# Handing over the recurrent states in the third quarter of six steps of a gated-attention and MLP kernel

## The chip, the core and the metric

The kernel runs on one core of a Trainium2 chip. The metric is the device time of one execution in microseconds. Several executions of each kernel are timed, and their median is what counts. A separate execution is recorded by the hardware profiler, and that is where the rows below come from.

## What is computed

The reference is a gated linear attention followed by an MLP with a SiLU:

```python
for t in range(S):
    state = alpha[:, :, t, :, None] * state + np.einsum('bhd,bhe->bhde', k[:, :, t], v[:, :, t])
    y[:, :, t] = np.einsum('bhd,bhde->bhe', q[:, :, t], state)
# x: y with its heads side by side, (B*S, H*D)
h = x @ w_in
g = h * (1.0 / (1.0 + np.exp(-h)))
out = g @ w_out
```

Here B = 4 batches, H = 8 heads, S = 768 time steps and D = 48. The MLP has 3072 tokens, a model width of 384 and an inner width of 2048. The weights come as 64-bit floating point numbers and are turned into 32-bit ones on the chip.

## The kernel before

**Chunks.** The time axis is cut into 6 chunks of 128 steps for each of the 4 batches, which makes 24 chunks (n = 0 to 23; n counts batches first, so chunk n + 4 continues chunk n). Each chunk goes through four stages:

- `products` (L710): transposes the chunk's decays, keys and queries on TensorE (L729), copies the decays (L731), and lets VectorE run what the prediction calls the chain: a scan (L734), the smallest decays (L737), the scaled keys kp (L745), a reciprocal (L762), a second scan (L764) and the scaled queries p (L770).
- `scores` (L792): kp times p on TensorE into two PSUM tiles, copied by ScalarE (L812) and masked by GpSimd (L813, in later steps L825); kp is also transposed into kn (L830, L832).
- `values` (L843): the masked scores g times v, and from the second chunk of a batch on p times the state, into a PSUM tile which ScalarE copies to `xt` (L863), the input of the MLP.
- `states` (L864): kn times v in 16 small matmuls (L874), put into the state of the batch: copied by ScalarE for a batch's first chunk (L882), added by VectorE afterwards (L880).

**Steps.** A loop (L1203) runs 25 steps of four quarters. In step s the quarters hold scores of chunk s-1, products of chunk s, values of chunk s-1 and states of chunk s-1. From step 8 on (`NA`) they are grouped differently. Behind states of chunk n two more things are issued: `load(n + 3)`, the decays, keys and queries of a later chunk (L477), and `load_v(n + 2)` (L501), both from SyncE's queue. Each quarter ends with `fill(step, slot)` (L1184), which lays down as much of the MLP's work as is due by then.

**The MLP's work** comes in pieces (generators). In the first steps these are `enter_plain` (L911), two column blocks of `x @ w_in` each, 6 matmuls into a `ps_m` bank and a Silu by ScalarE (L923); later `leave` (L1035), which multiplies by w_out and by differences of its blocks (`wt`). Ahead of pieces, `fill` has the weights converted: `weights` (L614) takes slices of 128 x 512 of w_in (12 slices) and 128 x 384 of w_out (16 slices). A slice's raw bits are fetched by SyncE's queue (L519) into one of four buffers, rounded by ScalarE (L629) and put together by VectorE in three instructions (L645, L646, L647). A new fetch is issued behind each conversion, and waits for its buffer.

**What sets the order.** The Python code gives a program order. A scheduler of the framework lays down, when the kernel is built, one fixed order for each engine: in program order by priority, but an instruction that it reckons ready may go ahead of one that it reckons is still waiting. On the chip each engine keeps to that order and waits on semaphores. Thus a stage that is moved in the program can change the order on all engines around it, also of instructions that the edit doesn't name. Matmul lines all show as L388, transposes as L392, because a small wrapper records them.

Of the kernel before, what the change touches and what calls it, by code (L numbers as in the profile page):

```python
# [355 lines left out]
def quotients(  # L356
# [98 lines left out]
    NA = 2 * GB  # L455
# [10 lines left out]
    def load(n, names="akq"):  # L466
        if n == NT:
            return
        c = ctxs.setdefault(n, dict(zip(("ci", "b"), divmod(n, B))))
        b, rows = c["b"], slice(c["ci"] * C, c["ci"] * C + C)  # L470
        for name, src in (("a", alpha), ("k", k), ("q", q)):
            if name not in names:
                continue
            x = src[b, :, rows, :]
            if n < NA:
                c[name] = nat[name][n % NIN]
                nc.sync.dma_start(c[name][:, :, 0:D], x.transpose([1, 0, 2]))  # L477
                continue

            c[name] = late["quads"][name]
            for u in range(2):
                for i in range(2):
                    r = 64 * u + 32 * i
                    nc.sync.dma_start(
                        c[name][r : r + 32, 32 * (1 - i) :][:, 0 : 4 * NP * D].rearrange(
                            "p (g c) -> p g c", g=NP),
                        x[u::2].rearrange("h (b j) d -> b h (j d)", j=4))
# [6 lines left out]
    def load_v(n):  # L496
        c = ctxs.setdefault(n, dict(zip(("ci", "b"), divmod(n, B))))
        x = v[c["b"], :, c["ci"] * C : c["ci"] * C + C, :].transpose([1, 0, 2])
        t = c["v"] = vns[n % NV]
        if n < NA:  # L500
            nc.sync.dma_start(t[:, :, 0:D], x)  # L501
            return
        nc.sync.dma_start(t[:, 0 : H // 2, 0:D], x[:, 0 : H // 2])
        for e in range(2):
            nc.sync.dma_start(t[CH * e : CH * e + CH, H // 2 :, 0:D], x[CH - CH * e : C - CH * e, H // 2 :])
# [665 lines left out]
    def settle():  # L1171

        first.close()
        late.update(look=pool("look"), part=pool("part"), turn=pool("turn"),
                    xc=pool("xc").tile([128, len(SUMS_X), TB], F32, name="xc"),
                    wx=pool("wx").tile([128, 8, NQ, 128], F32, name="wx"))
        quads = pool("quads")
        late["p"] = pool("p").tile([128, NP * W + 1], F32, name="p")
        late["quads"] = {name: quads.tile([128, 32 + 4 * NP * D], F32, name=f"{name}t") for name in "akq"}
        for name, t in late["quads"].items():  # L1180
            gps.memset(t, 1.0 if name == "a" else 0.0)
        load(NA)

    def fill(step, slot):  # L1184

        at = step * SLOTS + slot
        if at < marks[0]:
            if at == SLOTS:
                next(conv[0])
            elif step >= 1:  # L1190
                convert(0, (at - SLOTS) * 3 // (marks[0] - SLOTS) + 1)
            return
        i = next(i for i, m in enumerate(marks[1:]) if at < m)
        a, b = [work_at[n] for n in ([0] + phases)[i : i + 2]]
        due = a + (b - a) * (at - marks[i] + 1) / (marks[i + 1] - marks[i])
        if at % 2 == 0 and step > 3 * GB + 2:
            next(audits, None)
        while work_at[done + 1] <= due and pieces[done][2] <= bridged:
            convert(0, 3 * (done // 2) + 6)
            convert(1, 3 * (done - 6) // 2)  # L1200
            go_on()

    for step in range(STEPS):  # L1203
        if step == 1:
            load(NIN)
        stages = [[(scores, 1)], [(products, 0)], [(values, 1)], [(states, 1)]]
        if step == 1:

            stages = stages[1::-1] + stages[2:]
        elif step >= NA:  # L1210
            stages = [[(land, 1), (scores, 1)], [(products, 0)], [(quotient, 0)],
                      [(values, 1), (states, 1), (flip, 0)]]
        for slot, group in enumerate(stages):
            for stage, lag in group:
                n = step - lag
                if not 0 <= n < NT:
                    continue
                stage(n)
                if stage is values:
                    bridged = n + 1  # L1220
                if stage is states and n + 1 + NIN < NA:
                    load(n + 1 + NIN)
                if stage is states and n + NV < NT:
                    load_v(n + NV)
            if step * SLOTS + slot == (NA + 1) * SLOTS - 1:
                x = decayed.rearrange("p (o i c) -> p o i c", o=2, c=C)
                for r, o in later:
                    gps.memset(x[r, o, :, 0:CH], 0.0)
            fill(step, slot)
            if step * SLOTS + slot >= NA * SLOTS - 1 and conv_done[1] == NFT and not late:  # L1230
                settle()
# [32 lines left out]
@with_exitstack  # L1264
def kernel(
    ctx: ExitStack,
    tc: tile.TileContext,
    q: bass.AP,
    k: bass.AP,
    v: bass.AP,  # L1270
    alpha: bass.AP,
    moe_w_in: bass.AP,
    moe_w_out: bass.AP,
    out: bass.AP,
):


    flag = ctx.enter_context(tc.tile_pool(name="flag", bufs=1))
    small = flag.tile([1, 1], I32, name="small")
    args = (q, k, v, alpha, moe_w_in, moe_w_out, out)  # L1280
    within = quotients(tc, small, *args)
    with tc.If(within < 1, label="general"):
        general(tc, *args)
# [30 lines left out]
```

## Time and profile before

| | us |
|---|---|
| median of 3 runs (556.4 to 557.57) | 556.86 |
| the profiled execution | 557.26 |
| its span, first to last instruction | 555.5 |
| TensorE matmuls busy | 541.4 (97%) |
| TensorE weight loads busy | 489.7 (88%) |
| VectorE busy | 445.4 (80%) |
| ScalarE busy | 208.5 (38%) |
| GpSimd busy | 76.1 (14%) |

The mean granted TensorE clock is 0.999. In the rows, PE is TensorE's matmuls, PEld its weight loads, DVE VectorE, ACT ScalarE, POOL GpSimd and SPq SyncE's queue of DMA issues. A row of the timeline gives the start in us from the span's start, the time in us, the engine, the line, the operation, the tiles written and read with their shapes, how many instructions were merged into it, and in brackets how long the engine stood idle before it and what released it. A row of the waits gives an engine, its tile and line, what it waited for, and the sum in us, the number of times and the longest. A matmul of 32-bit numbers shows as two records, so 6 matmuls are a row of x12 and 16 of x32.

### The profile page before, as it was taken

The page shows a single profiled execution, that of the slowest core. Times are in us where ns is not written, and L with a number is a line of the kernel's source. Part 1 is how long each engine was busy: PE and PEld are TensorE (multiplying, and loading weights), DVE is VectorE, ACT ScalarE, POOL GpSimd, SP SyncE. Part 2 cuts the span into 40 slices and gives each one's busy share as a digit, 9 for nine tenths or more (in the row PEclk, how much of TensorE's full clock was granted, in tenths as well). Part 3 has the DMA queues.
Part 4 walks back from the last instruction along what each step waited for, and adds up shares of the span by engine and source line. Part 5 has one row for each costly group of instructions (what it writes and reads, how often), then busy time and mean ns, then how long its engine had stood idle before and what let it go on. Part 6 is the DMA issues. An engine that isn't in the chain of part 4 may idle for free. (4 is left out here: it accounts for less than half of the span.)

```text
span 555.5 us, 12640 instructions
## 1 busy us (share of the span) xinstructions
PE 541.4 (97%) x5026; PEld 489.7 (88%) x5026; DVE 445.4 (80%) x801; ACT 208.5 (38%) x466; POOL 76.1 (14%) x146
## 2 busy tenths in 40 slices
PE   6999999999999999999999999999999999999996
PEld 4788887998899999899999999988998999999996
DVE  5897788974999899997998986998884796945431
ACT  2556653223333253353353353344263342332100
POOL 3210000222210212021011021021121000001000
PEclk9999999999999999999999999999999999999999
DMA  9998971164454625355545654617642135500000
GB/s 215 246 249 210 232 195 33 47 161 116 117 136 125 159 63 138 86 145 149 139 112 139 193 139 120 191 27 183 170 137 91 54 91 169 172 11 22 10 24 30
DMA packets 99217, 70.09 MB, mean 126 GB/s; under 512 B 56272, under 2 KB 88656, under 8 KB 99152
## 3 DMA queue, kind: packets, MB, share of 16 engines
q1 hardware_dynamic: 97232, 65.30, 45.1%
q0 software_dynamic: 1920, 3.93, 2.0%
q8 instruction: 40, 0.66, 0.5%
q14 instruction: 25, 0.20, 0.1%
HBM read 61.34 MB, written 7.86 MB: 125 GB/s over the span
## 5 line engine op out<-in xcount | busy, mean ns | idle before, releaser
L388 PE MATMUL ps_o<-w_out,g 128*128 128x192 f32 x768 | 134.0, 328 | 0.5 <-DVE o L1056 0.5
L388 PEld LDWEIGHTS ps_o<-w_out,g 128*128 128x128 f32 x768 | 125.6, 190 | 3.5 <-DVE o L1056 1.0
L388 PE MATMUL ps_m<-xt,w_in 128*128 128x256 f32 x480 | 113.6, 383 | 1.5 <-ACT xt L863 1.1
L388 PEld LDWEIGHTS ps_m<-xt,w_in 128*128 128x128 f32 x480 | 89.1, 190 | 14.4 <-ACT xt L863 1.6
L388 PE MATMUL ps_o<-wt,g 128*128 128x192 f32 x576 | 99.7, 326 | 0.0
L388 PEld LDWEIGHTS ps_o<-wt,g 128*128 128x128 f32 x576 | 95.1, 190 | 1.6 <-issue 0.2
L388 PE MATMUL ps_m<-xc,w_in 128*128 128x256 f32 x288 | 70.7, 382 | 0.0
L388 PEld LDWEIGHTS ps_m<-xc,w_in 128*128 128x128 f32 x288 | 53.7, 190 | 7.0 <-DVE g L958 0.3
L1047 DVE TENSOR_TENSOR g<-g 128x512 f32<-128x512 f32 x72 | 50.1, 709 | 8.3 <-PE ps_o L388 8.3
L955 ACT ACTIVATE g<-g 128x1024 f32<-128x1024 f32 x32 | 33.1, 1056 | 61.2 <-DVE g L958 61.1
L1059 POOL DMA_DIRECT2D out_dram<-o x40 | 22.0, 551 | 219.5 <-DVE o L1056 113.7
L825 POOL TENSOR_SCALAR_AFFINE_SELECT g<-g 64x256 f32<-64x256 f32 x64 | 34.9, 546 | 124.4 <-ACT g L818 105.7
L388 PE MATMUL ps_m<-xc,wx 128*128 128x256 f32 x192 | 50.1, 383 | 1.0 <-DVE xc L586 1.0
L950 ACT COPY g<-ps_m 128x512 f32<-128x512 f32 x64 | 36.6, 588 | 37.0 <-PE ps_m L388 36.9
L388 PEld LDWEIGHTS ps_m<-xc,wx 128*128 128x128 f32 x192 | 35.2, 190 | 5.2 <-ACT u L1078 1.2
L958 DVE TENSOR_TENSOR g<-ps_m,g 128x512 f32<-128x512 f32 x56 | 37.1, 683 | 3.2 <-PE ps_m L388 2.7
L734 DVE TENSOR_TENSOR_SCAN u<-al,one 128x516 f32<-128x516 f32 x24 | 29.8, 1240 | 11.9 <-ACT al L731 11.6
L923 ACT ACTIVATE g<-ps_m 128x512 f32<-128x512 f32 x32 | 19.1, 597 | 41.7 <-PE ps_m L388 41.4
L950 ACT COPY part<-ps_m 128x512 f32<-128x512 f32 x32 | 18.9, 590 | 38.0 <-PE ps_m L388 24.0
L697 DVE TENSOR_REDUCE seen<-bits 128x1 f32<-128x512 int32 (+1 forms) x33 | 26.3, 823 | 5.7 <-DMA bits<-in_moe_w_in_dram 5.7
L764 DVE TENSOR_TENSOR_SCAN p<-al,inv 128x516 f32<-128x516 f32 x24 | 29.9, 1247 | 1.0 <-PE ps_a L388 0.3
L1056 DVE TENSOR_TENSOR o<-ps_o,u 128x192 f32<-128x192 f32 x24 | 8.5, 355 | 25.7 <-PE ps_o L388 22.8
(129 smaller groups left out, 648.5 us busy)
## 6 DMA issues: line engine op xcount, KB each, us to landing
bits<-in_moe_w_in_dram SPq DMA_DIRECT2D x24, 512.0 KB, 4.7
bits<-in_moe_w_out_dram SPq DMA_DIRECT2D x16, 384.0 KB, 3.9
at<-in_alpha_dram SPq DMA_DIRECT2D x64, 96.0 KB, 2.5
kt<-in_k_dram SPq DMA_DIRECT2D x64, 96.0 KB, 2.6
qt<-in_q_dram SPq DMA_DIRECT2D x64, 96.0 KB, 2.7
bits<-in_alpha_dram SPq DMA_DIRECT2D x9, 512.0 KB, 4.0
out_dram<-o POOLq DMA_DIRECT2D x40, 96.0 KB, 2.4
flips<-turn SPq DMA_DIRECT2D x12, 256.0 KB, 2.4
```

Of the source, the lines that this page charges most:

```text
L388: in_order(nc.tensor.matmul(*args, **kw))
L697: dve.tensor_reduce(seen[kind][which][:, i : i + 1], x, axis=AX, op=op, apply_absolute_value=True))
L734: dve.tensor_tensor_scan(u[:, end - 1 :: -1], sg[:, end:0:-1], one[:, end:0:-1], 0.0, ALU.mult, ALU.add)
L764: dve.tensor_tensor_scan(p[:, 0:end], sg[:, 0:end], iv[:, 0:end], 0.0, ALU.mult, ALU.add)
L825: gps.affine_select(x, x, pattern=[[0, NP], [1, CH]], compare_op=ALU.is_ge, fill=0.0, base=0, channel_multiplier=-1)
L923: act.activation(gts[grp, h, pair][:, i : i + 2, q % 2, :], ps, AF.Silu)
L950: act.copy(to, ps)
L955: act.activation(x, x, AF.Silu)
L958: dve.tensor_tensor(to, a, b, op)
L1047: dve.tensor_tensor(cells(grp, h, pair, *to), cells(grp, h, pair, *x), cells(grp, h, pair, *y), ALU.subtract)
L1056: dve.tensor_tensor(o, x, y, ALU.add)
L1059: (gps if grp < NG - 1 else nc.sync).dma_start(out[r : r + C, c * HO : (c + 1) * HO], o)
```

## The change

From the third to the eighth step (steps 2 to 7, counted from 0), the stage `states` and the loads behind it are moved from the last quarter of the step into the third, directly behind `values` of the same chunk and ahead of that quarter's `fill`. The last quarter then holds its `fill` alone. Step 0 is covered by the condition too, but has neither of the two stages; step 1 and the steps from 8 on are as they were.

```diff
@@ -1207,6 +1207,8 @@
         if step == 1:
 
             stages = stages[1::-1] + stages[2:]
+        elif step < NA:
+            stages = stages[0:2] + [stages[2] + stages[3], []]
         elif step >= NA:
             stages = [[(land, 1), (scores, 1)], [(products, 0)], [(quotient, 0)],
                       [(values, 1), (states, 1), (flip, 0)]]
```

The prediction numbers steps from 0, as the code does.

## Prediction, written before the changed kernel was run

> **What bounds the kernel now.** I read the page first (busy times, clock), then the waits of PE, then the first 110 us of the timeline engine by engine, because the edit touches nothing but steps 2 to 7 (counted from 0, as in the code), which lie there.
>
> ```profile
> PE 541.4 (97%) x5026; PEld 489.7 (88%) x5026; DVE 445.4 (80%) x801; ACT 208.5 (38%) x466; POOL 76.1 (14%) x146
> ```
>
> The waits of PE (what it waited for: us in total, times, longest):
>
> ```profile
> PE ps_m L388 <- ACT xt L863: 1.1, 4, 0.3
> PE ps_a L388 <- DVE kp L745: 0.5, 1, 0.5
> ```
>
> PE is busy 541.4 of 555.5 us, and of the 14.1 us it is not, 4.2 us are the first load and about 4 us the tail. So the end moves by what PE stands still more or less, and little else. Now PE in steps 2 and 3:
>
> ```profile
> 24.26 2.86 PE L388 MATMUL ps_m<-xt,w_in 128*128 128x256 f32 x12 [0.26 <-ACT xt L863]
> 27.05 0.27 PE L388 MATMUL ps_a<-vn,kn 128*32 128x48 f32 x2
> 27.25 2.86 PE L388 MATMUL ps_m<-xt,w_in 128*128 128x256 f32 x12
> ...
> 38.21 1.08 PE L388 MATMUL ps_a<-g,vn 128*32 128x128 f32 x32
> 39.22 2.86 PE L388 MATMUL ps_m<-xt,w_in 128*128 128x256 f32 x12
> 42.01 0.55 PE L388 MATMUL ps_a<-vn,kn 128*32 128x48 f32 x32
> ...
> 46.86 2.75 PE L388 MATMUL ps_m<-xt,w_in 128*128 128x256 f32 x12
> ```
>
> Each x12 row is one piece of the first MLP product: 6 matmuls, shown as 12 records, 2.79 us start to start (0.465 us each). The row at 39.22 is the first piece that reads w_in's third quarter of columns, hence converted slices 6, 7 and 8 of w_in (12 slices, in order; one matmul in three reads each). DVE makes these slices with three instructions each (L645, L646, L647), and between them computes each chunk's decays, L734 to L770, which I call the chain:
>
> ```profile
> 33.46 0.69 DVE L647 CUSTOM_DVE_ANT_0 w_in<-w_in,up 128x1024 uint16<-128x1024 uint16 x1 [0.35 <-ACT up L629]
> ...
> 35.36 0.69 DVE L647 CUSTOM_DVE_ANT_0 w_in<-w_in,up 128x1024 uint16<-128x1024 uint16 x1
> ...
> 36.30 1.23 DVE L734 TENSOR_TENSOR_SCAN u<-al,one 128x516 f32<-128x516 f32 x1
> ...
> 38.70 0.68 DVE L647 CUSTOM_DVE_ANT_0 w_in<-w_in,up 128x1024 uint16<-128x1024 uint16 x1
> ...
> 46.80 0.69 DVE L647 CUSTOM_DVE_ANT_0 w_in<-w_in,up 128x1024 uint16<-128x1024 uint16 x1
> 50.76 1.23 DVE L734 TENSOR_TENSOR_SCAN u<-al,one 128x516 f32<-128x516 f32 x1 [3.26 <-ACT al L731]
> 54.85 0.35 DVE L645 TENSOR_SCALAR w_out<-bits 128x384 int32<-128x384 int32 x1
> ```
>
> The four L647 rows end slices 6, 7, 8 and 11. Slice 8 is finished at 39.38, when PE's piece, begun at 39.22, needs it at about 40.15: weights arrive just in time, with under 1 us to spare. An undisturbed chain lasts 54.85 - 50.76 = 4.09 us. It starts when ACT has copied the transposed decays (L731), behind a Silu:
>
> ```profile
> 34.41 0.60 ACT L923 ACTIVATE g<-ps_m 128x512 f32<-128x512 f32 x1 [0.42 <-PE ps_m L388]
> 34.91 0.58 ACT L731 COPY al<-ps_a 128x512 f32<-128x512 f32 x1
> ```
>
> And SyncE's queue, which fetches weights (bits) and chunks (an, kn, qn, vn):
>
> ```profile
> 24.77 6.51 SPq L519 DMA_DIRECT2D bits<-in_moe_w_in_dram  x4
> 31.37 0.39 SPq L477 DMA_DIRECT2D an<-in_alpha_dram  x1
> ...
> 37.07 1.29 SPq L519 DMA_DIRECT2D bits<-in_moe_w_in_dram  x2
> ```
>
> The x4 row holds the transfers of slices 6 to 9; chunk 4's four loads keep the queue from 31.37 to 37.07, 5.7 us.
>
> **What the Trainium skill says.** "Perfetto Trace Analysis", Identifying the Most-Contended Engine: matmul busy time is a poor measure, weight-load time a better one; here both agree (97% and 88%). "TensorE: Matmul & The Clock Gate", HAM oscillation: only idle gaps beyond about 3.4 us cool the clock. In this trace the granted clock is 1.00 in every 10 us after gaps of 0.5 us, so I charge a gap of under 2 us its own length alone; no run here shows such a gap. "DMA: Bandwidth & Descriptors", Queues, rings and completion order: descriptors of one ring are consumed in ring order, so a load issued ahead of a weight transfer delays it; the trace agrees (landing took 3.6 to 6.1 us for bits between 20 and 62 us).
>
> **The change part by part.** No instruction is added or removed; the stages states, load and load_v of steps 2 to 7 come before the third quarter's filler instead of after it. What moves is in the built order of each engine, which I compared.
>
> (1) PE, split states. In steps 2, 4 and 6 the old order lays the 16th states matmul behind one or two pieces (the row at 27.05, and at 57.92 and 93.44). Alone it costs 27.25 - 27.05 = 0.20 us; as the 16th of a run about 0.03, which lies under the wait for xt (0.26 to 0.30 us) that follows. New order: 16 in a row. Three times 0.20 = -0.6 us. In steps 3, 5 and 7 all 16 move whole ahead of the fill: 0.
>
> (2) DVE in step 3, the costly part. In the new order chunk 3's whole chain stands ahead of slice 7; before it was woven around slice 8. Worked out: PE is 0.20 early after step 2's split, so the Silu of 34.41 and the copy behind it end at 34.91 + 0.58 - 0.20 = 35.29. Slice 6 is done by 34.15, so DVE waits 1.1 us and the scan starts at 35.33. Chain to 39.42. Then slice 7: L645 0.45, L646 0.60, an L1033 that stands in between 0.60, L647 0.69: ends 41.76 (before: 36.05). Slice 8 has L645, L646, slice 9's L645 and then its own L647: 2.0 us more, 43.8 (before: 39.38).
> PE meanwhile: values of chunk 2 at 38.21 - 0.20 = 38.01, 0.89 us (53.45 to 54.34 in step 4), states 0.48 (42.01 to 42.49), so 39.38. The new order starts two pieces at once, one matmul of each (0.93 us, slice 6): 40.31. The third matmul needs slice 7: idle till 41.78, **1.47 us**. Then two matmuls and five of the eight score matmuls (0.93 + 0.68): 43.4. The next needs slice 8: **0.38 us**. The rest (8 matmuls 3.72, three scores 0.4, transposes 0.5) ends at 48.4, where the next piece starts instead of at 46.86; slice 11, at 48.9, is ready before its matmul at 49.4. Sum +1.85 us.
> Late next: chunk 4's chain. DVE had 3.26 us of idle ahead of it and takes the 1.4 us out of that, so it follows PE, as does everything behind it.
>
> (3) SP. Chunk 4's loads stand ahead of slices 7 to 9, so slice 7's transfer goes out some 3.8 us later: 25.3 + 5.7 = 31.0 instead of 27.27. With 3.6 to 6.1 us it lands at 34.6 to 37.1. Needed at 38.6 by the rounding L629, which ACT now has behind the next Silu (38.32 + 0.60 - 0.20), and at 39.42 by DVE: 0, hidden under the chain. If that cover goes, every further microsecond is a microsecond of PE. Later weight transfers wait for slots that conversions free (L646), as before: 0. In step 8 v's load goes ahead of at's; that may shorten DVE's 1.45 us wait for at, but the query it leads to is done at 125.66 and read by PE at 129.67: 0.
>
> (4) ACT. The state copies (L882, 0.63 us a pair) move by a few instructions; their readers come a chunk later: 0. In step 5 one rounding is laid ahead of a Silu and the score copies. By DVE's pace (1.56 us a slice) it makes them up to 0.7 us later; GpSimd's mask follows, and I reckon it done 0.2 us before PE's values of step 6. The Silu ahead of L1033 and the scan slips about 0.1 us, and that chain is what PE's 0.51 us wait for kp (87.22) hangs on: +0.1 us.
>
> (5) DVE, L880 (0.36 us, two a step). Ahead of conversions in step 5, which leaves 1.67 us of idle at 82.7 as cover; in step 6 ahead of the w_out work, where two were already; in step 7 states need kp's buffer (L745, done 105.71) at 106.28: 0.57 us to spare. All 0; without the cover 0.7 us.
>
> Sum: +1.85 - 0.6 + 0.1 = **+1.35 us**. From step 8 on the order of every engine is the same but for v/at and two memsets, and PE's later waits (0.48 at 143.8, 0.39 at 229, 0.96 at 368, 0.51 at 532) all hang on work PE itself released, so I carry the shift to the end undiminished. The profiled execution took 557.26 us for a span of 555.5 and would take 558.6; it was 0.4 above the median of the runs, 556.86, which gives **558.2 us**.
>
> Bounds. The stall of (2) is no wait that the old trace shows. Below: if slice 7 ended by 40.3 there is none and the sum is -0.5 us. Above: with the chain hindered (GpSimd's L813 stretched one L646 from 0.69 to 1.02) or weights landing late, another 1.5 us. I take the middle, since every duration in it is from rows of the same stage.
>
> **Rivals.**
> A, the forecast: +1.35 us, own range 557.5 to 558.9.
> B, wash: the stall is smaller, about 0.6 us, because the chain starts sooner, or a later DVE wait absorbs part of it. For: those waits sum to 2.3 us. Against: DVE is itself idle for PE between them (7.63 us at 139.2). 556.9 us.
> C, ending on the other side: the stall is not there and the three splits pay, 0.5 us, 556.3 us. It decides at slice 7 done at 40.3: the chain would have to start 1.45 us earlier, at 33.9, but the transposes it reads come at 34.0 at the earliest. Thin.
> D, more: the transfers behind chunk 4's loads or step 6's mask and kp miss their slack (1.4, 0.2, 0.6 us) as well. For: DMA is full there (slices of 9 tenths up to 60 us). +2.5 us, 559.4 us.
>
> **How the numbers follow.** A 0.58, B 0.15, C 0.07, D 0.20. A measurement of this kernel can tell about 0.2% from no change, 1.1 us: slower is beyond 557.97. A lies past that two times in three: slower 0.38 + 0.20 = 0.58; within 0.2 + 0.15 = 0.35; faster 0.07. The range leaves out C with a little of B below, and the far part of D above: 556.9 to 559.9.
>
> **What would show it.** Right: in the changed profile PE has two new waits for DVE w_in L647 between 40 and 44 us, of about 1.5 and 0.4 us; DVE idles about 1.1 us ahead of the scan near 35.3; no x2 states rows remain; from 60 us on PE's rows stand 1.2 to 1.5 us later than before. Wrong: slice 7's bits landing after 39, a gap for POOL g ahead of step 6's values, or a shift that shrinks after 130 us.

## The result and the profile after

The changed kernel took 557.39 us (median of 19 executions, 556.55 to 558.53) against 556.64 us for the kernel before on the same chip (19 executions): a ratio of 1.0016 with a 95% interval from 1.0008 to 1.0023, that is +0.9 us (+0.45 to +1.3; the medians themselves differ by 0.75). It is slower, as forecast, and by 0.46 us less than the +1.35 us of the sum. The time lies within the range of 556.9 to 559.9, but just under forecast A's own range (557.5 to 558.9), and under the 557.97 from which the prediction would have called a kernel slower: by its own line this is the case "within", to which it gave 0.35. Of the 0.8 us below 558.2, 0.2 us is the kernel before (556.64 in 19 executions, 556.86 in the three known then). With 19 executions of each kernel, the interval lies wholly on the slower side all the same.

The profiled execution of the changed kernel has a span of 555.1 us, 0.4 us *below* that of before. That is no contradiction: the openings of the two executions differ (last section). In the changed kernel's profile the first MLP piece starts at 22.93 us, in that of before at 24.26. Below, times are therefore taken from the start of the first piece, and totals from the medians alone.

The page's busy times after:

```profile
PE 538.5 (97%) x5026; PEld 488.6 (88%) x5026; DVE 446.9 (81%) x801; ACT 208.5 (38%) x466; POOL 77.0 (14%) x146
```

The waits of PE after (us in total, times, longest). The first line is new, the second had one wait of 0.5 before:

```profile
PE ps_m L388 <- DVE w_in L647: 1.3, 1, 1.3
PE ps_a L388 <- DVE kp L745: 0.8, 2, 0.5
```

The timeline of PE after, steps 2 to 4:

```profile
22.93 5.45 PE L388 MATMUL ps_m<-xt,w_in 128*128 128x256 f32 x24 [0.26 <-ACT xt L863]
28.30 1.16 PE L388 MATMUL ps_a<-p,kp 48*128 48x128 f32 x16
...
37.83 1.13 PE L388 MATMUL ps_m<-xt,w_in 128*128 128x256 f32 x4
40.28 1.13 PE L388 MATMUL ps_m<-xt,w_in 128*128 128x256 f32 x4 [1.32 <-DVE w_in L647]
41.34 0.93 PE L388 MATMUL ps_a<-p,kp 48*128 48x128 f32 x10
42.28 3.72 PE L388 MATMUL ps_m<-xt,w_in 128*128 128x256 f32 x16
45.94 0.71 PE L388 MATMUL ps_a<-p,kp 48*128 48x128 f32 x6
47.07 2.76 PE L388 MATMUL ps_m<-xt,w_in 128*128 128x256 f32 x12
```

Three things are to be seen. The last of step 2's 16 states matmuls no longer stands between the first two pieces (x24 in one row). PE then stops for 1.32 us after one matmul of each of two pieces, for slice 7. And the scores now stand in two runs, x10 and x6, between matmuls of the pieces, where before they were one run behind them.

VectorE and SyncE at that place:

```profile
33.79 1.23 DVE L734 TENSOR_TENSOR_SCAN u<-al,one 128x516 f32<-128x516 f32 x1 [0.70 <-ACT al L731]
...
39.54 0.69 DVE L647 CUSTOM_DVE_ANT_0 w_in<-w_in,up 128x1024 uint16<-128x1024 uint16 x1
...
41.55 0.68 DVE L647 CUSTOM_DVE_ANT_0 w_in<-w_in,up 128x1024 uint16<-128x1024 uint16 x1
```

```profile
29.57 0.91 SPq L501 DMA_DIRECT2D vn<-in_v_dram  x1
30.59 8.85 SPq L519 DMA_DIRECT2D bits<-in_moe_w_in_dram  x5
```

Behind slice 6 (done at 33.08) come chunk 3's whole chain, slice 7 (done at 40.23), slice 8 (42.23): the order that the prediction read. Behind step 2's states four loads are issued: the decays, keys and queries of chunk 4, and v of chunk 3, which the prediction counts as chunk 4's too. The last of them is shown; they stand ahead of the fetches of slices 7 to 9, whose first goes out at 30.59 (before: 27.27).

### The profile page after: what moved, and what is told of

It reads as the page before. It is cut to its first block, busy times and chain, and to the rows that moved or that the text cites. A ratio compares the mean times of both kernels' runs of the same rounds, so it can differ in the third digit from the quotient of the medians.

```text
span 555.1 us, 12640 instructions
## 1 busy us (share of the span) xinstructions
PE 538.5 (97%) x5026; PEld 488.6 (88%) x5026; DVE 446.9 (81%) x801; ACT 208.5 (38%) x466; POOL 77.0 (14%) x146
## 5 line engine op out<-in xcount | busy, mean ns | idle before, releaser
L923 ACT ACTIVATE g<-ps_m 128x512 f32<-128x512 f32 x32 | 19.1, 598 | 40.6 <-PE ps_m L388 40.2
```

Of the source, the lines that this page charges most:

```text
L923: act.activation(gts[grp, h, pair][:, i : i + 2, q % 2, :], ps, AF.Silu)
```

## The experiments

Each edit is shown against the kernel before or the changed kernel, as said. The us in the table are worked out from the measured ratio to the kernel before on the same chip (what it has over 1, times 557 us), with the 95% interval. The differences of the medians lie within about 0.3 us of them, but for e7, which ran five times: its medians differ by 2.85 us.

| kernel | step 2's loads | us | interval |
|---|---|---|---|
| the change | early | +0.9 | +0.45 to +1.3 |
| e2 loads alone | early | +2.1 | +1.3 to +2.9 |
| e3 step 2 alone | early | +1.3 | +0.9 to +1.8 |
| e7 chunk 3's chain behind slices 7, 8 | early | +2.4 | +1.6 to +3.1 |
| e1, e8 states alone (twice) | late | 0.0, -0.1 | -0.6 to +0.45 |
| e5 all but step 2's loads | late | -0.6 | -1.1 to -0.2 |
| e4, e9 steps 3 to 7 (twice) | late | -0.8, -0.8 | -1.2 to -0.3 |
| e10 steps 3 to 7, loads late | late | -0.1 | -0.5 to +0.45 |
| e6 steps 3 to 6 | late | -0.3 | -0.7 to +0.1 |
| e11 steps 4 to 7 | late | -0.6 | -1.1 to 0.0 |

The table parts in two: all four kernels with step 2's loads in the third quarter are slower than before, and none of the eight runs of the others is.

**First batch: states or loads, step 2 or the later ones.** The theory was the prediction's: the chain ahead of slice 7 costs, the unsplit runs of states gain. The rival was that the moved states themselves cost, or that steps 3 to 7 do.

The states moved, the loads left in the fourth quarter of each step (e1, against the changed kernel):

```diff
-                if stage is states and n + 1 + NIN < NA:
-                    load(n + 1 + NIN)
-                if stage is states and n + NV < NT:
-                    load_v(n + NV)
+                if stage is states and not 2 <= step < NA:
+                    if n + 1 + NIN < NA:
+                        load(n + 1 + NIN)
+                    if n + NV < NT:
+                        load_v(n + NV)
+            if slot == 3 and 2 <= step < NA:
+                n = step - 1
+                if n + 1 + NIN < NA:
+                    load(n + 1 + NIN)
+                load_v(n + NV)
```

> The states stage moves as in the change, but the loads behind it (load, load_v) stay in the fourth quarter of steps 2 to 7. Theory (the cost comes from the moved loads of step 2, which put chunk 4's transfers ahead of three weight slices, so that the built order puts chunk 3's chain ahead of slice 7; the moved states only gain): PE has no wait for DVE w_in L647, the three split states runs are gone, about 0.4 us each (two profiles: 5.78 against 5.38 us from one piece to the scores), one new wait of 0.3 us for kp in step 7: -0.9 us against the kernel before, about 555.8 where that has 556.7. Rival (the moved states matmuls themselves delay the pieces): slower, like the full change, +0.9 us.

Measured: 557.20 us against 557.48, ratio 1.0000 (0.9991 to 1.0008). The stall in step 3 is gone, the gain is missing. The timeline of PE shows a new wait in its place: 0.98 us at 47.40 us, in step 4, for the last slice of w_in (slice 11). It is followed up below (e5, e8).

The loads of decays, keys and queries moved, the states and v's load left in the fourth quarter (e2, against the kernel before):

```diff
-                if stage is states and n + 1 + NIN < NA:
-                    load(n + 1 + NIN)
-                if stage is states and n + NV < NT:
-                    load_v(n + NV)
+                if stage is states and not 2 <= step < NA:
+                    if n + 1 + NIN < NA:
+                        load(n + 1 + NIN)
+                    if n + NV < NT:
+                        load_v(n + NV)
+                if stage is values and 2 <= step < NA:
+                    if n + 1 + NIN < NA:
+                        load(n + 1 + NIN)
+            if slot == 3 and 2 <= step < NA:
+                load_v(step - 1 + NV)
```

> The states stage stays in the fourth quarter; only load, the decays, keys and queries of the later chunk, moves to the third quarter in steps 2 to 7. Theory (the moved loads cost): the stall in step 3 as in the full change (1.3 to 1.8 us of PE waiting for DVE w_in L647), the splits of states remain and with a further one in step 3: +1.5 to +2.0 us against the kernel before. Rival (the moved states cost): no stall, within 0.3 us of before.

Measured: 559.30 us, +2.1 us (ratio 1.0038, 1.0024 to 1.0052), just above the +1.5 to +2.0 us that were expected. Here v's load stayed late, so the loads of decays, keys and queries are enough. The timeline of PE has the changed kernel's stall for slice 7, 1.29 us at 40.24 us, without the gains.

The change in step 2 alone (e3), and in steps 3 to 7 alone (e4), against the changed kernel:

```diff
-        elif step < NA:
+        elif step == 2:
             stages = stages[0:2] + [stages[2] + stages[3], []]
```

```diff
-        elif step < NA:
+        elif 3 <= step < NA:
             stages = stages[0:2] + [stages[2] + stages[3], []]
```

> The change in step 2 alone (states and loads). Theory: the whole stall (about +1.6 us), one split removed (-0.4 us): +1.2 us against before, more than the full change's +0.9. Rival (the cost builds up over the steps, each a little): a sixth of the change, +0.2 us.

> The change in steps 3 to 7, not in step 2. Theory: no stall in step 3, two splits removed (-0.8 us), whole states runs in steps 3 and 5 (-0.2), a new wait for kp in step 7 (+0.3): -0.7 us against before. Rival (cost builds up over the steps): +0.7 us.

Measured: 558.73 us (+1.3) and 556.37 us (-0.84). Both came out as expected. With step 2 alone PE waits 0.99 us for slice 7 at 40.26 us; with steps 3 to 7 none, and in step 3 the two pieces run through (5.45 us from 39.86 us).

So the whole loss comes from step 2, and there (e1 against e2) from the loads. The closest comparison is that of the change with e5 below, whose edit differs in the place of step 2's loads alone: +0.9 us against -0.6 us, each to the kernel before on its own chip. The loss shows a step later, in step 3, where the prediction had placed it without naming step 2 as its source.

**Second batch: the order on VectorE or the late fetch.** Two things happen together when step 2's loads go early: the fetches of slices 7 to 9 are issued later, and the built order on VectorE puts the chain ahead of slice 7. Kernel e7 is the changed kernel with slices 7 and 8 put ahead of the chain again:

```diff
-        dve.tensor_tensor_scan(u[:, end - 1 :: -1], sg[:, end:0:-1], one[:, end:0:-1],
-                               0.0, ALU.mult, ALU.add)
+        scan = dve.tensor_tensor_scan(u[:, end - 1 :: -1], sg[:, end:0:-1], one[:, end:0:-1],
+                                      0.0, ALU.mult, ALU.add)
+        if n == 3:
+            tc.keep_in_program_order(scan)
```

> The whole change, but chunk 3's scan keeps its place in the program order, so that slices 7 and 8 stand ahead of chunk 3's chain on VectorE; chunk 4's loads still go ahead of slices 7 to 9. If the order of VectorE alone makes the stall, PE no longer waits for L647 and the time is about -0.8 us against before. If the late fetches alone bind, slice 7 is rounded at 37.8 us all the same; it is then done at 38.5 to 39.1 and slice 8 at 40.5 to 41.1, PE waits about 1.2 us for slice 8 and up to 0.4 us more for chunk 3's p, and the time stays 0.5 to 1.0 us above before.

Measured: 559.88 us, +2.4 us, more than either reading said, and far from the -0.8 us of the order alone. VectorE waits for the fetch, then for a Silu's output:

```profile
35.74 0.43 DVE L645 TENSOR_SCALAR w_in<-bits 128x512 int32<-128x512 int32 x1 [1.45 <-DMA bits<-in_moe_w_in_dram]
...
38.53 0.69 DVE L1035 TENSOR_TENSOR g<-g 128x512 f32<-128x512 f32 x1 [1.64 <-ACT g L925]
```

(L1035 and L925 are the lines L1033 and L923, two lower in this file.) ScalarE at that place:

```profile
37.90 0.60 ACT L925 ACTIVATE g<-ps_m 128x512 f32<-128x512 f32 x1 [2.83 <-PE ps_m L388]
38.39 0.73 ACT L629 ACTIVATE up<-bits 128x512 int32<-128x512 uint32 x1
```

Slice 7's bits are there at 35.74, when VectorE starts on them, but ScalarE rounds them only at 38.39: in its own fixed order this rounding stands behind a Silu that waits for PE until 37.90. In the kernel before, the rounding of slice 7 stood ahead of the Silu (two roundings from 32.72, the Silu at 34.41). So e7 turned back VectorE's order and left ScalarE's, and it changed PE's order too: four matmuls now stand ahead of the stall, and the scores are one run.

PE pays in five places:

```profile
42.24 3.72 PE L388 MATMUL ps_m<-xt,w_in 128*128 128x256 f32 x16 [1.11 <-DVE w_in L647]
46.42 1.16 PE L388 MATMUL ps_a<-p,kp 48*128 48x128 f32 x16 [0.46 <-DVE p L772]
...
52.75 4.15 PE L388 MATMUL ps_m<-xt,w_in 128*128 128x256 f32 x18 [0.41 <-DVE w_in L647]
```

With the two rows left out, 0.49 us for a score copy at 49.41 and 0.27 for w_in at 50.11, the sum is 1.11 + 0.46 + 0.49 + 0.27 + 0.41 = 2.74 us. Of the two built orders, the one with the chain first is the faster: in e7 VectorE stands idle for 1.45 and 1.64 us where the changed kernel works on the chain.

So e7 does not part the late fetch from the orders around it. As an estimate, VectorE needs about 2.0 us for a slice (before: slice 7 from 34.07 to 36.05), so with the bits at 35.74 slice 7 could have been done near 37.7 us, and PE comes to it at 39.14 + 0.93 = 40.07. The late landing alone then need not have stopped PE for slice 7. In e2, on the other hand, ScalarE rounds slice 7 at 35.03, in good time, and the slice is still done only at 40.18, behind the chain, and PE stalls. What is shown is that step 2's early loads stop PE, with either order on VectorE. That they do so because the scheduler reckons slice 7's bits late and lays other work ahead of them, on VectorE and on ScalarE, is argued. A kernel with the late fetches and the order of before on both engines was not tried.

**What became of step 2's unsplit states.** Kernel e5 is the changed kernel with the loads of step 2 alone left in the fourth quarter. Against the kernel of steps 3 to 7 its order on PE differs by one thing, the unsplit run of step 2.

```diff
-                if stage is states and n + 1 + NIN < NA:
-                    load(n + 1 + NIN)
-                if stage is states and n + NV < NT:
-                    load_v(n + NV)
+                if stage is states and step != 2:
+                    if n + 1 + NIN < NA:
+                        load(n + 1 + NIN)
+                    if n + NV < NT:
+                        load_v(n + NV)
+            if slot == 3 and step == 2:
+                load(step + NIN)
+                load_v(step - 1 + NV)
```

Kernel e8 is e1 once more.

> The change, but in step 2 the loads stay in the fourth quarter; states are moved in all six steps. Against the kernel of steps 3 to 7 it differs on PE by one thing: step 2's 16 states matmuls run unsplit. If moved states only gain, it is 0.4 us below that kernel, about -1.2 us against before, with no wait of PE for L647 between 36 and 46 us. If the conversions of w_in are a floor that ends near 47.4 us, PE waits for slice 11 in place of it: no better than steps 3 to 7 alone (-0.8), or back at 0 as with the states alone.

> The kernel with the states moved and all loads left, once more. If its 0.0 us was a true loss of the expected 0.9 us, it comes again within 0.4 us and its profile shows a wait of PE for slice 11 near 47 us; if that profile's wait came from its early opening, the wait is smaller where the opening is later, and the time lies at -0.5 to -1.0 us.

Measured: e5 556.47 us (-0.6), not the -1.2 us of a pure gain but near the floor's -0.8; e8 556.91 us (-0.1), so the miss of e1 was no accident. All three profiles show the wait for slice 11 (0.97 to 1.01 us), also where the first piece begins late (e5: 24.27 us). PE of e5, in step 4:

```profile
48.19 1.99 PE L388 MATMUL ps_m<-xt,w_in 128*128 128x256 f32 x8 [1.01 <-DVE w_in L647]
```

VectorE of e5 never stands idle for more than 0.14 us from the scan at 22.20 us to the end of slice 11 at 48.13:

```profile
22.20 1.23 DVE L734 TENSOR_TENSOR_SCAN u<-al,one 128x516 f32<-128x516 f32 x1 [1.79 <-ACT al L731]
...
31.86 0.86 DVE L645 TENSOR_SCALAR w_in<-bits 128x512 int32<-128x512 int32 x1
32.76 1.00 DVE L646 SCALAR_TENSOR_TENSOR w_in<-bits,w_in 128x512 int32<-128x512 int32 x1
```

So in steps 2 to 4 of this profile VectorE's work is a floor, and the 0.40 us that PE saves in step 2 is spent waiting for slice 11. It even comes later than before: from the first piece 23.86 us, in the kernel before 23.24. About 0.2 us of that is slice 6: its first two rows, shown last above, took 0.86 and 1.00 us where 0.42 and 0.69 are usual (before, 0.42 and 1.02 and then a wait of 0.35). Another 0.2 us is slice 11's last instruction, with 0.90 us where 0.69 are usual. GpSimd's mask (L813) runs beside the first two from 31.55 to 33.21. The Trainium skill ("SBUF — State Buffer", Who interferes with whom) says that a VectorE instruction with two inputs in SBUF, such as L646, contends with a GpSimd instruction that reads SBUF, and names tensor_scalar, the kind of L645, among those that can contend in a two-port mode. Here both took longer beside the mask; whether L645 runs in such a mode no run shows.

The floor does not account for the times, though. e5 has the wait for slice 11 and is at -0.6 us, while e1 and e8 have it and are at 0. Nor does e5's profile show where its -0.6 us come from: it is of the slowest of its 16 executions (557.88 us), and from the first piece to the last matmul it took 0.41 us more than the profile of before. What takes the gain from e1 is taken up next (e10).

**The other steps.** Three kernels ask what the moves of steps 3 and 7 and the loads behind step 2 are worth: steps 3 to 6 alone (e6), steps 3 to 7 with all loads late (e10), steps 4 to 7 alone (e11). Kernel e9 is e4 again, on the chip of e10 and e11. The edits, against the changed kernel (e6, e11; e10 has e4's condition, and e1's loads with 3 in place of 2):

```diff
-        elif step < NA:
+        elif 3 <= step < NA - 1:
```

```diff
-        elif step < NA:
+        elif step in (4, 5, 6, 7):
```

> The change from step 3 to step 6 alone, steps 2 and 7 as before. If the wait for kp in step 7 (0.28 us) is the price of step 7's move, it is gone, and the time is about -1.1 us against before; if that wait is paid by work that PE would have waited for later anyway, -0.8 us as with steps 3 to 7.

> The change from step 3 on, as measured before at -0.84 us, once more. If that gain is real it comes again within 0.4 us (-0.4 to -1.2 us against before); if the few tenths between the kernels without a stall are scatter of the openings, it may as well come out between -0.5 and 0.

> States moved in steps 3 to 7, with all loads left in the fourth quarter. The order on TensorE and VectorE is that of the kernel of steps 3 to 7; on SyncE's queue alone chunks' loads stand a few weight fetches later. If the loads' place costs nothing from step 3 on, the time is that of the kernel of steps 3 to 7 (within 0.4 us). If late loads are what took the gain from the kernel with the states alone, it is 0.5 to 0.8 us above it, at about 0 against before; and then step 2's states are not to blame.

> The change from step 4 on; step 3 as before, in which the 16 states matmuls stand unsplit between two pieces. It prices step 3's move: if only splits of the run of 16 cost, 0 to 0.1 us above the kernel of steps 3 to 7; if every run of states between two pieces costs a switch there and back, 0.2 to 0.4 us above it. In both cases no wait of PE for L647 over 0.5 us.

Measured: e9 555.94 us (-0.8, so that gain is real), e6 556.81 (-0.3), e10 556.78 (-0.1), e11 556.51 (-0.6).

e6 met neither number: leaving step 7 out was no gain, and its wait for kp of 0.28 us is not a price worth avoiding. Its interval overlaps that of e4, so nothing more follows.

e10 has the same order on PE, VectorE and ScalarE as e9, and yet came out 0.7 us higher on the same chip. The two intervals overlap by a little, so this difference is likely and not certain. It fits the second case of e10's expectation: the loads of steps 3 to 7, left late, take the gain, here and in e1 and e8, and step 2's states are not to blame. e5, which leaves only step 2's loads late and keeps most of the gain, fits it too. So by the times the loads are likely better early from step 3 on, while in step 2 they are better late.

Where e10 loses it the profiles don't show. In step 6 its PE stands idle ahead of the values:

```profile
84.81 1.08 PE L388 MATMUL ps_a<-g,vn 128*32 128x128 f32 x32 [0.36 <-issue]
```

This looks like a cost of the late loads, since e9 has no such gap. But e4, which is e9's kernel, has it too, with 0.33 us at 84.84. From the first piece to these values it is 60.15 us in e9, 60.28 in e4 and 60.48 in e10, and to the end of the last matmul 525.6, 526.2 and 525.9 us. The two profiles of one kernel differ by as much as e10 differs from either.

e11 cannot be told from e9 by its time, but the profile prices step 3's move. PE of e11, then of e9:

```profile
36.71 1.08 PE L388 MATMUL ps_a<-g,vn 128*32 128x128 f32 x32
37.72 2.86 PE L388 MATMUL ps_m<-xt,w_in 128*128 128x256 f32 x12
40.51 0.55 PE L388 MATMUL ps_a<-vn,kn 128*32 128x48 f32 x32
...
43.77 1.16 PE L388 MATMUL ps_a<-p,kp 48*128 48x128 f32 x16
```

```profile
36.96 1.08 PE L388 MATMUL ps_a<-g,vn 128*32 128x128 f32 x32
37.86 0.52 PE L388 MATMUL ps_a<-vn,kn 128*32 128x48 f32 x32
38.31 5.45 PE L388 MATMUL ps_m<-xt,w_in 128*128 128x256 f32 x24
43.69 1.16 PE L388 MATMUL ps_a<-p,kp 48*128 48x128 f32 x16
```

The same matmuls take 43.77 - 36.71 = 7.06 us with the states between two pieces, and 43.69 - 36.96 = 6.73 us with them behind the values: 0.33 us for a whole run of 16, unsplit.

The kernel of steps 3 to 7 beats both kernels, by 0.8 us (before) and, through the kernel before, by 1.7 us (after).

## Why the prediction was right

**The stall** was there, at its place and near its size. From the first piece, slice 7 was done after 17.30 us (forecast 41.76 - 24.26 = 17.50), slice 8 after 19.30 (forecast 19.54), and PE waited 1.32 us (forecast 1.47). VectorE idled 0.70 us ahead of the scan (forecast 1.1). The second wait of 0.38 us is not there: the five score matmuls ahead of it took 0.93 us and not 0.68, and by then slice 8 was done. The seventh piece starts 24.14 us after the first, before 22.60: +1.54 us. The working, which has it at 48.4, gave +1.54 as well; by the sum it is +1.85 - 0.20 = +1.65, so the two are not quite of one piece. That the first agrees to the hundredth is luck: slice 8 came 0.24 us earlier than forecast, and the rest took 0.24 us longer.

**Its cause** was put a step too near. The loads on SyncE (3) were costed at nothing, hidden under the chain, and the whole loss was put on the order of VectorE (2). In the changed kernel as built no wait for the fetch does show: VectorE turns to slice 7 at 37.88, right behind the chain, and the bits were there near 35.5 (an estimate: in e7 they were fetched at 30.85 and there at 35.74, here they were fetched at 30.59). But e3, e4 and e5 show that the moves of step 2, and of them its loads, make the stall that step 3 shows: with these loads late it is gone. The forecast had this price in its sum all the same, because it was worked out from the built order, in which the loads' effect already stood.

**The switches of PE** were mis-sized, and this is the term behind the 0.46 us. The split state matmul was priced by the start of the next row, 0.20 us. Step 2's rows say 30.04 - 24.26 = 5.78 us from the first piece to the scores before and 28.30 - 22.93 = 5.37 after (5.38 in e5): 0.40 us. And a run moved whole, costed at 0, saves 0.33 (e9 against e11). The shift along PE follows this step by step: +1.54 at the seventh piece, +1.14 at chunk 4's scores (step 4's split, -0.40), +0.81 at chunk 5's (step 5's run, -0.33), +0.46 at chunk 6's (step 6's split, -0.35), +0.59 at chunk 7's. In step 3 itself such a gain buys nothing, because there VectorE's slices hold PE: e3, in which step 3 is as before, waits 0.99 us instead of 1.32, and its seventh piece stands at +1.55.

**Carrying the shift undiminished** failed therefore: 1.2 to 1.5 us were forecast from 60 us on, and 0.8 stood there, 0.5 to 0.6 by 112 us. The reason is not rival B's later waits taking it up, but the gains of steps 4 to 6. From there to the end it does hold: +0.81 at PE's last matmul. Of the rise from 0.59, 0.3 comes between 359 and 380 us after the first piece, where two profiles of one kernel, e4 and e9, differ by more than that, so nothing follows from it.

**Of (4) and (5)**, the mask of step 6 was no gap in the changed kernel, as said, though the slack was as thin as forecast: e4 and e10 have a gap of 0.33 and 0.36 us at that place. In step 7 the wait for kp, costed at 0 with 0.57 us to spare, was 0.27 us.

Rival C, faster by 0.5 us, did not come about, but it is what the same edit gives without step 2, by more. Rival D's added misses did not come. Of rival B's two grounds, neither holds (the stall was 1.32 us, and no later wait took it up), although the time lies nearer to its 556.9 than to 558.2.

Two slips of the working cost nothing. 38.32 + 0.60 - 0.20 is 38.72 and not 38.6; and landing times of 3.6 to 6.1 us do not show that loads ahead delay a fetch. That shows in the issue, at 30.59 instead of 27.27.

## What to carry to other kernels

When a stage is moved, look first at the transfers it issues and at what stands behind them in that queue: here four loads, issued a quarter of a step earlier, cost more than all the moved arithmetic gained, and the cost appeared a step later on other engines. Then read the built order of every engine that handles those transfers: putting VectorE's order back alone did not help, since ScalarE's rounding stood behind a wait of its own. Ask of each saved stretch whether the engine beside it can follow: in e5's profile TensorE's 0.40 us in step 2 bought only a longer wait, since VectorE was busy with hardly a gap. Price a small group of matmuls by the distance between the groups around it with and without it, not by its own row.

## What the runs showed of the hardware

**A switch between groups of matmuls had a price.** One states matmul of 32x48 shape laid between two pieces cost 0.40 us (5.78 against 5.38 us for the same pieces), a run of 16 laid there 0.33 us more than the same run behind the values (7.06 against 6.73). What makes this price no run shows.

**Two VectorE instructions took longer beside GpSimd's mask.** In e5 L645 took 0.86 us instead of 0.42 and L646 1.00 instead of 0.69 while L813 ran.

**The opening differs from execution to execution.** In the first 24 us TensorE was slow for stretches of different lengths. The same scores (16 records) near 11 us took 2.08 us in the profile of before, 1.85 after and 1.16 in e4. In e4 the granted clock read 0.66 on average from 14 to 24 us and 1.00 from there to 60. In the profile of before it read 1.00 all along, also where the scores took 2.08 us, so there the clock is not shown to be the cause. The first piece began anywhere between 22.76 us (e11) and 24.56 us (e4). The Trainium skill ("TensorE: Matmul & The Clock Gate", Part 1: The HAM clock gate) says that the window in which activity is counted runs freely and isn't set back by the start of a kernel, so that the slow stretch at the start varies; the varying openings agree with that, and no run here tests it. The executions of one kernel spread over some 2 us, as much as the openings.

**A short stop left the clock as it was.** After the stall of 1.32 us the granted clock stayed at 1.00 (40 to 50 us), as the prediction had taken it.
